# Turning sums and later batches' x on VectorE in 32x32 blocks, in an attention and feed-forward kernel written by a planner

## The chip, the cores and the metric

The kernel runs on one core of one Trainium2 chip. The metric is the device time in microseconds (us). A core has TensorE (PE; matmuls, its weight loads are shown as PEld), VectorE (DVE), ScalarE (ACT), GpSimd (POOL) and a queue SP that here only issues DMAs. Matmul results land in PSUM, in banks of 512 fp32 columns; everything else lives in SBUF, which has 128 partitions.

## The reference

The input x has 4 batches of 12480 tokens with 128 channels; there are 32 inducing points. The second part is a feed-forward block with 2048 hidden units over all 49920 tokens.

```python
def mab(q, kv):
    s = scale * (q @ kv.transpose(0, 2, 1))
    s = s - s.max(-1, keepdims=True)
    a = np.exp(s)
    a /= a.sum(-1, keepdims=True) + 1e-09
    return a @ kv
h = mab(I, x)          # 32 inducing points attend to all tokens of a batch
y = mab(x, h)          # every token attends to those 32 results
...
h = np.maximum(y @ w_in, 0.0)
out = (h * h @ w_out)
```

## The kernel before

**Tiling.** A unit is 960 tokens (UNIT), 13 units to a batch, 52 in all; a block is half a unit, 480 tokens (BLK). A unit of x is loaded with tokens on 120 partitions, 8 rows of 128 channels on each (tile xn).

**The first attention** (class First). TensorE turns x into channels by tokens, four transposes of 120 tokens for each block (tile xtp in PSUM, L463), and ScalarE or VectorE copies the result to SBUF (tile xt). Then come the first scores (L478), maximum, exponential, a turn of the weights (ep, L512), and the mix with xn (nb, L536), which is added up over the batch with a running maximum. The units of batch 0 are handled before the main part ("early"). The 39 units of batches 1 to 3 are handled inside the main part, each of them 13 units before it is needed.

**The second attention** (class Second) gives each token its weights over the 32 points: scores from xt (na, L674), a copy to SBUF (ss), a turn (s2t, L693), maximum, exponential, sum, division, a turn back (ap, L752). The high part (sw, rounded to fp32r) and the rest are copied out of PSUM, and 16 small DMAs spread them over 128 partitions as the stack st, tokens of a block lying every second 120 of it.

**The feed-forward** (ffn_block). The product of h with w_in is made once per batch (hw), so the hidden units come straight from st: 16 matmuls of 128 x 480 per block (tile h, L896). ScalarE makes relu (L908) and square (L924) into g. VectorE splits g into a rounded part hi (L929) and a rest lo (L934). TensorE then adds hi times wo_hi, hi times wo_lo and lo times wo_hi into one PSUM bank op (L973), 48 matmuls per block. The sum op holds channels by tokens. It is copied to SBUF (ot, by either engine), turned on TensorE in four transposes (otp, L993), copied by VectorE into osb, and a whole unit is stored by one DMA with 4 KB runs. The last block of all is handled in two halves.

**What sets the order.** Nothing is issued as it is written. `add` puts each step into a Plan with an engine (or a choice, "ACT|DVE"), a cost in ns, a due time, what it needs, and the buffers it takes. `Plan.run` goes through the steps as a list scheduler and issues the instructions in that order, so each engine's order is fixed. SP's waits are in its own order too. PERIOD is the planned time of a unit; it spaces the due times.

**PSUM.** Four banks hold h, two hold op (tag o), and two (tag m) are shared by all small products: xtp, na, nb, ep, s2t, ap and otp.

Of the kernel before, what the change touches and what calls it, by code (L numbers as in the profile page):

```python
# [11 lines left out]
F32 = mybir.dt.float32  # L12
# [10 lines left out]
NT = 8  # L23
UNIT = TS * NT
BLK = UNIT // 2


class Task:
# [135 lines left out]
def induced_attention_then_squared_relu_ffn(  # L164
# [16 lines left out]
    scale = 1.0 / math.sqrt(C)  # L181
    NQ = NF // 4
    GB, HB, LB = 3, 2, 2
    PERIOD, START, T_MAIN, NARROW, STEP = 32000.0, 2600.0, 44000.0, -9000.0, 3000.0
    W_DUE = [14e3, 20e3, 28e3, 34e3, 50e3, 52e3, 56e3, 60e3]

    XT, OT, ST = ("ACT|DVE", "ACT|DVE"), ("ACT|DVE", "ACT|DVE"), "ACT|DVE"
# [2 lines left out]
    ORDER = "x0 x1 x2 i0 x3 x4 x5 i1 x6 x7 x8 i2 x9 x10 i3 x11 x12 o0 o1 o2 o3".split()  # L190
    SPARE = (6, 7, 8)
    FIRST_PAIRS, LAST_PAIRS = 2, 1
    OB, SS, SS_NS = "DVE", "DVE", 317

    FUSED = set()
    POOL_HI = set()
# [4 lines left out]
    HALVES = True  # L201
    PATIENCE = (0.0, 0.0, 40.0)

    PAIR, PAIR_DUE, XTP_PAIR = False, 3000.0, False
    MB = 2
    G1_DUE, SQ_DUE, HI_DUE, LO_DUE, OP_DUE = -2000.0, 6000.0, 5000.0, 6000.0, 10500.0
    WIDE_LATER, NEXT_FIRST, STEP_0 = 7000.0, 2000.0, 600.0
# [4 lines left out]

    const = ctx.enter_context(tc.tile_pool(name="const", bufs=1))
    xn_pool = ctx.enter_context(tc.tile_pool(name="xn", bufs=3))
    xt_pool = ctx.enter_context(tc.tile_pool(name="xt", bufs=NU + 1))
    hw_pool = ctx.enter_context(tc.tile_pool(name="hw", bufs=2))
    att = ctx.enter_context(tc.tile_pool(name="att", bufs=2))
# [1 line left out]
    ps_h = ctx.enter_context(tc.tile_pool(name="ps_h", bufs=2, space=PSUM))  # L219
    ps_o = ctx.enter_context(tc.tile_pool(name="ps_o", bufs=4 - MB, space=PSUM))  # L220
    ps_m = ctx.enter_context(tc.tile_pool(name="ps_m", bufs=MB, space=PSUM))
    plan = Plan(dict(xn=3, early=6, xt=NU + 1, m=MB, h=2, o=4 - MB, g=GB, hi=HB, lo=LB, st=2, sw=2), T_MAIN, STICK, PATIENCE)

    def bank(name):
        return ps_m.tile([P, 512], F32, tag="m", name=name)


    x_v = x.rearrange("b (p j) c -> b p j c", p=TS)
    out_v = out.rearrange("(b p j) c -> b p j c", b=B, p=TS)

    def load_x(b, u, pool):
        xn = pool.tile([TS, NT, C], F32, tag="xn", name=f"xn_{b}_{u}")
        nc.sync.dma_start(xn, x_v[b, :, u * NT:(u + 1) * NT, :])
        return xn

    ind_sb = const.tile([M, C], F32, name="ind_sb")
# [32 lines left out]
    def copy(task, dst, src):  # L269
        ENG[task.by](dst, src)  # L270
# [137 lines left out]
    class First:  # L408
        def __init__(self, b, u, due, early=False, begun=None):

            self.b, self.u, self.early, self.n, self.begun = b, u, early, f"{b}_{u}", begun
            self.s = s = state.setdefault(b, {"xt": {}, "chain": None, "bxt": {}})
            self.home = "early" if early and u not in SPARE else "xn"
            self.bx = Buffer(self.home)
            self.bt = s["bxt"][u] = Buffer("xt")
            lead = 2500 if early else 8000

            def load():
                self.xn = (pools["early"] if self.home == "early" else xn_pool).tile(
                    [TS, NT, C], F32, tag="xn", name=f"xn_{self.n}"  # L420
                )
                nc.sync.dma_start(self.xn, x_v[b, :, u * NT:(u + 1) * NT, :])

            loaded = add("SP", 2050, load, ORDER.index(f"x{u}") * 10.0 - 1000.0 if b == 0 else due - lead - 20000, takes=[self.bx], late=0)
            self.turned = []
            if XTP_PAIR and not early:
                self.turn_both(due - lead, loaded)
                return
            for k in range(2):
                self.turned.append(self.turn(k, due - lead + k * lead * 0.4, loaded))  # L430

        def turn_both(self, due, loaded):
            banks = [Buffer("m"), Buffer("m")]
            tp = {}

            def turn():
                self.xt = self.s["xt"][self.u] = xt_pool.tile([C, UNIT], F32, tag="xt", name=f"xt_{self.n}")
                for k in range(2):
                    tp[k] = bank(f"xtp_{self.n}_{k}")
                    for t in range(4):  # L440
                        nc.tensor.transpose(tp[k][:, t * TS:(t + 1) * TS], self.xn[:, 4 * k + t, :], ident[:TS, :TS])

            t = state["turn"] = add("PE", 750, turn, due, [loaded, state.get("turn"), self.begun], mode="t",
                                    takes=banks + [self.bt], reads=[self.bx])
            for k in range(2):
                def turned(k=k):
                    copy(self.turned[k], self.xt[:, k * BLK:(k + 1) * BLK], tp[k][:, :BLK])

                self.turned.append(add(XT[k], (440, 567), turned, due + XT_DUE, [t], reads=[banks[k], self.bt]))

        def turn(self, k, due, loaded):
            bank_ = Buffer("o" if self.early else "m")
# [212 lines left out]
    class Second:  # L665
# [13 lines left out]
        def weigh(self, scored, where, bank_, due, step, pair=None):  # L679
# [119 lines left out]
            if first:  # L799
# [5 lines left out]
                for k in range(2):  # L805
# [2 lines left out]
                    last = add(ST, (455, 565), lambda k=k: stacked1(k), d + (5 + k) * step, [t, last],  # L808
                               takes=[] if k else [self.bst], reads=[ba] + ([self.bst] if k else []))
                    t1.append(last)  # L810
                self.ready = t1
                return
            t = add("PE", 219, back, d + 4 * step, [tp], takes=[ba], mode="t")
            th = add(ST, (255, 317), high, d + 5 * step, [t], takes=[bw], reads=[ba])
# [60 lines left out]
    def ffn_block(b, u, k, second, t0, g_open, by_pairs, fused, bulk):  # L875
# [7 lines left out]
        def quad(j, last):  # L883
# [4 lines left out]
            for i in range(2):  # L888
# [3 lines left out]
                def wide(l, i=i, c=c):  # L892
                    if l == 0:
                        c["hp"] = ps_h.tile([P, 2, 512], F32, tag="h", name=f"h_{n}_{2 * j + i}")
                    f = 4 * j + 2 * i + l
                    nc.tensor.matmul(  # L896
                        c["hp"][:, l, :BLK].rearrange("p (q t) -> p q t", q=Q), s["hw"][:, f * P:(f + 1) * P], s["st", u][:, :, k, :],
                        start=True, stop=True,
                    )

# [82 lines left out]
        for j in range(NQ):  # L983
            last = quad(j, last)

        def done():
            w["ot"] = att.tile([P, BLK], F32, tag="ot", name=f"ot_{n}")
            copy(td, w["ot"], w["op"][:, :BLK])

        def turn():  # L990
            w["tp"] = tp = bank(f"otp_{n}")
            for q in range(Q):
                nc.tensor.transpose(  # L993
                    tp[:TS, q * P:(q + 1) * P], w["ot"][:, q * TS:(q + 1) * TS], ident
                )

        def turned():
            if k == 0:
                s["osb", u] = att.tile([TS, NT, C], F32, tag="osb", name=f"osb_{b}_{u}")

            copy(
                tt, s["osb", u].rearrange("t (q k) c -> t k q c", k=2)[:, k],
                w["tp"][:TS, :].rearrange("t (q c) -> t q c", q=Q),
            )

        def store():
            nc.sync.dma_start(out_v[b, :, u * NT:(u + 1) * NT, :], s["osb", u])

        def store_block():
            pair = out_v[b, :, u * NT:(u + 1) * NT, :].rearrange("t (q k) c -> t k q c", k=2)  # L1010
            nc.sync.dma_start(pair[:, k], s["osb", u].rearrange("t (q k) c -> t k q c", k=2)[:, k])

        end = t0 + PERIOD / 2 + 8000
        if HALVES and (b, u) == units[-1] and k == 1:

            for h in range(2):
                def done_h(h=h):
                    if h == 0:
                        w["ot"] = att.tile([P, BLK], F32, tag="ot", name=f"ot_{n}")
                    c = slice(h * 2 * TS, (h + 1) * 2 * TS)  # L1020
                    ENG["ACT" if h else "DVE"](w["ot"][:, c], w["op"][:, c])

                def turn_h(h=h):
                    w["tp", h] = tp = bank(f"otp_{n}_{h}")
                    for q in range(2):
                        nc.tensor.transpose(
                            tp[:TS, q * P:(q + 1) * P], w["ot"][:, (2 * h + q) * TS:(2 * h + q + 1) * TS], ident
                        )

                def rows(x, h=h):  # L1030
                    return x.rearrange("t (q k) c -> t k q c", k=2)[:, k, 2 * h:2 * h + 2]

                def turned_h(h=h, rows=rows):
                    ENG["ACT" if h else "DVE"](
                        rows(s["osb", u]), w["tp", h][:TS, :2 * P].rearrange("t (q c) -> t q c", q=2)
                    )

                def store_h(rows=rows):
                    nc.sync.dma_start(rows(out_v[b, :, u * NT:(u + 1) * NT, :]), rows(s["osb", u]))

                bt = Buffer("m")
                e = "ACT" if h else "DVE"
                t = add(e, 300, done_h, end + h, [last], reads=[bo], late=0)
                t = add("PE", 219, turn_h, end + 600, [t], takes=[bt], mode="t")
                t = add(e, 330, turned_h, end + 1500, [t], reads=[bt], late=0)
                add("SP", 1500, store_h, end + 6000, [t])
            return w["begun"]
        bt = Buffer("m")
        td = add(OT[k], (455, 570), done, end + OT_DUE, [last], reads=[bo], late=LATE_OT)
        t = add("PE", 437, turn, end + OTP_DUE, [td], takes=[bt], mode="t")  # L1050
        t = tt = s["out", u, k] = add(OB, (480, 600), turned, end + OSB_DUE, [t], reads=[bt])
        if (b, u) == units[-1]:
            add("SP", 1500, store_block, end + 6000, [t])
        elif k == 1:
            add("SP", 2000, store, end + 6000, [t, s["out", u, 0]])
        return w["begun"]


# [73 lines left out]
```

## Time and profile before

| what | value |
|---|---|
| time, median of three runs | 1729.77 us (1728.26 to 1730.32) |
| profiled execution, its span | 1730.0 us |
| TensorE busy | 1706.0 us, 99% |
| VectorE busy | 1651.4 us, 95% |
| ScalarE busy | 1605.6 us, 93% |
| GpSimd busy | 58.3 us, 3% |
| DMA | 82.06 MB in 56935 packets; 18.1% of 16 engines |

The span is the time of the one execution that the profiler recorded. Busy is the time in which an engine had an instruction running; overlapping records count once. Idle time is put down to whatever ended it, the releaser. In a group, "out<-in" are the program's tile names, x is a count, then come busy microseconds and the mean duration in nanoseconds of one instruction. Copies by the helper all have line L270, so they are told apart by tile.

### The profile page before, as it was taken

The numbers are of one execution on the slowest core, as the hardware profiler recorded it, in microseconds if no ns is written. First come the engines' busy times: TensorE is split into PE (matmuls) and PEld (weight loads), VectorE is DVE, ScalarE is ACT, GpSimd is POOL, SyncE is SP. The second block draws the span as 40 slices with busy tenths as digits, with TensorE's granted clock in tenths as the row PEclk, the third lists the DMA queues.
The fourth block names the chain that finished last, engine by engine and source line by source line (L and its number), as shares of the span: only waits on it lengthen the run. The fifth ranks groups of instructions, "written<-read, shape, count | busy, mean of one in ns | idle before, by whom it ended". The sixth has DMA issues, their size and how long they took to land.

```text
span 1730.0 us, 25326 instructions
## 1 busy us (share of the span) xinstructions
PE 1706.0 (99%) x9527; PEld 1416.2 (82%) x9527; DVE 1651.4 (95%) x1734; ACT 1605.6 (93%) x1686; POOL 58.3 (3%) x57
## 2 busy tenths in 40 slices
PE   7899999999999999999999999999999999999998
PEld 5588888888788888888878888888887888888887
DVE  5999999999999999999999999999999999999998
ACT  6699999999989999999988999999998999999997
POOL 0000000000000000000000000000000000000000
PEclk9899999999999999999999999999999999999999
DMA  9121111111121111111212111111110111111010
GB/s 234 51 55 47 51 43 44 52 45 43 36 57 47 50 43 46 52 45 43 53 29 58 49 43 47 51 44 44 42 28 24 35 35 40 30 37 33 24 46 23
DMA packets 56935, 82.06 MB, mean 47 GB/s; under 512 B 14790, under 2 KB 43942, under 8 KB 56814
## 3 DMA queue, kind: packets, MB, share of 16 engines
q1 hardware_dynamic: 56814, 80.46, 18.1%
q8 instruction: 75, 1.23, 0.3%
q14 instruction: 46, 0.38, 0.1%
HBM read 29.77 MB, written 25.56 MB: 32 GB/s over the span
## 4 chain that ended last, share of the span: by engine, by line
PE 94%; DVE 2%; ACT 1%; DMA 1%; SPq 1%; issue 0%; ACTq 0%; DVEq 0%
PE op L973 61%; PE h L896 21%; PE otp L993 3%; PE xtp L463 2%; PE na L674 2%; PE nb L536 1%; PE na L478 1%; PE ep L512 1%; PE s2t L693 1%; PE ap L752 1%; PE wp L632 1%; DVE lo L934 0%; SPq L768 0%; DVE hi L929 0%; PE sp L478 0%
## 5 line engine op out<-in xcount | busy, mean ns | idle before, releaser
L934 DVE TENSOR_TENSOR lo<-g,hi 128x1920 fp32r<-128x1920 f32 (+1 forms) x419 | 895.2, 2137 | 16.8 <-DVE hi L929 0.5
L908 ACT ACTIVATE g<-h 128x960 f32<-128x960 f32 x832 | 794.7, 983 | 62.5 <-PE h L896 60.8
L924 ACT ACTIVATE g<-g 128x1920 f32<-128x1920 f32 (+1 forms) x419 | 758.8, 1811 | 4.0
L896 PE MATMUL h<-st,hw 128*128 128x480 f32 x1664 | 523.5, 392 | 2.4 <-DMA st<-sw 1.2
L929 DVE CAST hi<-g 128x1920 fp32r<-128x1920 f32 (+1 forms) x419 | 480.0, 1146 | 20.0 <-PE op L973 9.6
L973 PE MATMUL op<-hi,wo_lo 128*128 128x480 f32 x1664 | 495.7, 383 | 0.0
L973 PE MATMUL op<-hi,wo_hi 128*128 128x480 f32 x1664 | 458.8, 386 | 0.0
L973 PE MATMUL op<-lo,wo_hi 128*128 128x480 f32 x1664 | 436.6, 382 | 0.0
L973 PEld LDWEIGHTS op<-lo,wo_hi 128*128 128x128 f32 x1664 | 311.4, 188 | 52.6 <-issue 1.0
L973 PEld LDWEIGHTS op<-hi,wo_lo 128*128 128x128 f32 x1664 | 308.9, 188 | 53.0 <-issue 4.6
L896 PEld LDWEIGHTS h<-st,hw 128*128 128x128 f32 x1664 | 303.0, 189 | 57.1 <-issue 11.7
L973 PEld LDWEIGHTS op<-hi,wo_hi 128*128 128x128 f32 x1664 | 304.1, 188 | 45.9 <-issue 0.9
L715 POOL TENSOR_SCALAR z<-z 120x8 f32<-120x8 f32 x51 | 57.6, 1130 | 1606.6 <-DVE z L711 1606.6
L270 DVE COPY osb<-otp 120x512 f32<-120x512 f32 x103 | 70.2, 682 | 0.1
L463 PE MATMUL xtp<-ident,xn 120*128 120x120 f32 x416 | 61.9, 276 | 4.3 <-DMA xn<-in_x_dram 3.6
L463 PEld LDWEIGHTS xtp<-ident,xn 120*128 120x128 f32 x416 | 51.2, 146 | 17.5 <-issue 3.7
L993 PE MATMUL otp<-ident,ot 128*120 128x128 f32 x412 | 61.8, 272 | 0.5 <-DVE ot L270 0.5
L993 PEld LDWEIGHTS otp<-ident,ot 128*120 128x120 f32 x412 | 50.4, 137 | 12.8 <-DVE ot L270 1.5
L270 ACT COPY xt<-xtp 128x480 f32<-128x480 f32 x71 | 40.3, 572 | 13.4 <-PE xtp L463 13.4
L270 ACT COPY ot<-op 128x480 f32<-128x480 f32 x65 | 37.1, 570 | 0.8 <-PE op L973 0.8
L536 PE MATMUL nb<-xn,et 120*32 120x128 f32 x752 | 34.1, 280 | 0.0
L674 PE MATMUL na<-xt,hT 128*32 128x240 f32 x416 | 32.7, 387 | 0.4 <-DVE hT L270 0.4
(117 smaller groups left out, 650.6 us busy)
## 6 DMA issues: line engine op xcount, KB each, us to landing
xn<-in_x_dram SPq DMA_DIRECT2D x52, 480.0 KB, 4.3
st<-sw SPq DMA_DIRECT2D x816, 30.0 KB, 1.9
out_dram<-osb SPq DMA_DIRECT2D x51, 480.0 KB, 3.4
hi_i<-in_moe_w_in_dram SPq DMA_DIRECT2D x2, 512.0 KB, 13.5
lo_i<-in_moe_w_in_dram SPq DMA_DIRECT2D x2, 512.0 KB, 15.6
hi_o<-in_moe_w_out_dram SPq DMA_DIRECT2D x2, 512.0 KB, 11.9
lo_o<-in_moe_w_out_dram SPq DMA_DIRECT2D x2, 512.0 KB, 9.8
out_dram<-osb SPq DMA_DIRECT2D x1, 240.0 KB, 2.6
```

Source lines behind the costliest of these rows:

```text
L270: ENG[task.by](dst, src)
L463: nc.tensor.transpose(v["tp"][:, t * TS:(t + 1) * TS], self.xn[:, 4 * k + t, :], ident[:TS, :TS])
L536: nc.tensor.matmul(where[q * M:(q + 1) * M, :], self.et[:, k, q * M:(q + 1) * M], self.xn[:, 2 * q + k, :], start=(k == 0), stop=(k == 1),)
L674: nc.tensor.matmul(where[q * M:(q + 1) * M, :], self.s["hT"][:, :M], self.s["xt"][self.u][:, q * 2 * TS:(q + 1) * 2 * TS], start=True, sto ...
L715: E.tensor_scalar(v["z"], v["z"], 1e-9, 0.0, ALU.add, ALU.add)
L896: nc.tensor.matmul(c["hp"][:, l, :BLK].rearrange("p (q t) -> p q t", q=Q), s["hw"][:, f * P:(f + 1) * P], s["st", u][:, :, k, :], start=Tr ...
L908: nc.scalar.activation(g, h, AF.Relu)
L924: nc.scalar.activation(v["g"][:, h], v["g"][:, h], AF.Square)
L929: ENG[by](v["hi"][:, h], v["g"][:, h])
L934: engine.tensor_sub(v["lo"][:, h], v["g"][:, h], v["hi"][:, h])
L973: nc.tensor.matmul(w["op"][:, :BLK], wo[:, 4 * j + l, :], v[name][:, l, :], start=(j == x == 0 and l == 0), stop=(j == NQ - 1 and x == 5 a ...
L993: nc.tensor.transpose(tp[:TS, q * P:(q + 1) * P], w["ot"][:, q * TS:(q + 1) * TS], ident)
```

## The change

1. VectorE turns op straight out of PSUM, in 32x32 blocks, into a tile ob (one instruction of 480 columns per block). The copies ot and osb, the transposes otp and their bank go. In ob, partition 32g + t, row r, holds 32 channels of group g of token 32r + t, so four DMAs, one for each group, store a block in runs of 32 channels (128 bytes).
2. For units of batches 1 to 3, x is loaded a second time, by four DMAs in runs of 128 bytes, into a tile xb (one buffer) with that same arrangement, and one VectorE instruction of 960 columns turns it into xt. The transposes xtp and their copies stay for batch 0 alone. The mix still reads xn.
3. Blocks of 32 tokens must be consecutive, so the order of tokens in a unit changes: xn is loaded with token j x 120 + p of the unit on partition p (runs of 512 bytes where they were 4 KB), and a block's tokens stand side by side in st, so a hidden product reads one run of 480 columns. The first unit's two blocks now both wait for both halves of its stack.
4. The copy ss of the second scores may go to ScalarE or VectorE.
5. PERIOD goes from 32000 to 30500 ns.

The last block's two halves are now two VectorE turns, of 256 and 224 columns, with four DMAs each. An unused variant (turn_both) goes.

```diff
+S = 32
+NR = BLK // S
...
-    PERIOD, START, T_MAIN, NARROW, STEP = 32000.0, 2600.0, 44000.0, -9000.0, 3000.0
+    PERIOD, START, T_MAIN, NARROW, STEP = 30500.0, 2600.0, 44000.0, -9000.0, 3000.0
...
-    OB, SS, SS_NS = "DVE", "DVE", 317
+    OB, SS, SS_NS = "DVE", "ACT|DVE", (255, 317)
...
+    xb_pool = ctx.enter_context(tc.tile_pool(name="xb", bufs=1))
...
-    x_v = x.rearrange("b (p j) c -> b p j c", p=TS)
-    out_v = out.rearrange("(b p j) c -> b p j c", b=B, p=TS)
+    xb_v = x.rearrange("b (u r t) (g c) -> b u g t r c", r=UNIT // S, t=S, c=S)
+    x_v = x.rearrange("b (u j p) c -> b u p j c", j=NT, p=TS)
+    out_v = out.rearrange("(b u k r t) (g c) -> b u k g t r c", b=B, k=2, t=S, r=NR, g=P // S)
...
-            if XTP_PAIR and not early:
-                self.turn_both(due - lead, loaded)
+            if not early:
+                self.turned.append(self.turn_blocks(due - lead))
                 return
...
+        def turn_blocks(self, due):
+            b, u = self.b, self.u
+            bb = Buffer("xb")
+            v = {}
+
+            def load():
+                v["xb"] = xb_pool.tile([P, UNIT // S, S], F32, tag="xb", name=f"xb_{self.n}")
+                for g in range(P // S):
+                    nc.sync.dma_start(v["xb"][g * S:(g + 1) * S], xb_v[b, u, g])
 
             def turn():
...
+                self.xt = self.s["xt"][u] = xt_pool.tile([C, UNIT], F32, tag="xt", name=f"xt_{self.n}")
+                nc.vector.transpose(self.xt, v["xb"].rearrange("p r c -> p (r c)"))
+
+            t = state["blocks"] = add("SP", 2050, load, due - 20000, [state.get("blocks")], takes=[bb], late=0)
+            t = state["turn"] = add("DVE", 1070, turn, due + XT_DUE, [t, state.get("turn"), self.begun], takes=[self.bt], reads=[bb])
+            return t
...
-                self.ready = t1
+                self.ready = [last] * 2
...
-                        c["hp"][:, l, :BLK].rearrange("p (q t) -> p q t", q=Q), s["hw"][:, f * P:(f + 1) * P], s["st", u][:, :, k, :],
+                        c["hp"][:, l, :BLK], s["hw"][:, f * P:(f + 1) * P],
+                        s["st", u][:, 2 * k:2 * k + 2].rearrange("p q k t -> p (q k t)"),
...
-        td = add(OT[k], (455, 570), done, end + OT_DUE, [last], reads=[bo], late=LATE_OT)
-        t = add("PE", 437, turn, end + OTP_DUE, [td], takes=[bt], mode="t")
-        t = tt = s["out", u, k] = add(OB, (480, 600), turned, end + OSB_DUE, [t], reads=[bt])
...
+        def turn(rows):
+            if "ob" not in w:
+                w["ob"] = att.tile([P, NR, S], F32, tag="ob", name=f"ob_{n}")
+            nc.vector.transpose(
+                w["ob"][:, rows].rearrange("p r c -> p (r c)"), w["op"][:, rows.start * S:rows.stop * S]
             )
...
+        def store(rows):
+            for g in range(P // S):
+                nc.sync.dma_start(out_v[b, u, k, g, :, rows], w["ob"][g * S:(g + 1) * S, rows])
...
+        parts = [slice(0, 8), slice(8, NR)] if (b, u) == units[-1] and k == 1 else [slice(0, NR)]
+        t = None
+        for rows in parts:
+            t = add("DVE", 70 + 500 * (rows.stop - rows.start) / NR, lambda rows=rows: turn(rows), end + OT_DUE, [last, t],
+                    reads=[bo], late=LATE_OT if len(parts) == 1 else 0)
+            add("SP", 2000, lambda rows=rows: store(rows), end + 6000, [t])
```

More of the change, by code (lines that the diff above doesn't have):

```diff
@@ L202, in induced_attention_then_squared_relu_ffn @@
     PATIENCE = (0.0, 0.0, 40.0)
-    PAIR, PAIR_DUE, XTP_PAIR = False, 3000.0, False
+    PAIR, PAIR_DUE = False, 3000.0
     MB = 2
@@ L221, in induced_attention_then_squared_relu_ffn @@
     ps_m = ctx.enter_context(tc.tile_pool(name="ps_m", bufs=MB, space=PSUM))
-    plan = Plan(dict(xn=3, early=6, xt=NU + 1, m=MB, h=2, o=4 - MB, g=GB, hi=HB, lo=LB, st=2, sw=2), T_MAIN, STICK, PATIENCE)
+    plan = Plan(dict(xn=3, xb=1, early=6, xt=NU + 1, m=MB, h=2, o=4 - MB, g=GB, hi=HB, lo=LB, st=2, sw=2), T_MAIN, STICK, PATIENCE)
     def bank(name):
         return ps_m.tile([P, 512], F32, tag="m", name=name)
-    x_v = x.rearrange("b (p j) c -> b p j c", p=TS)
-    out_v = out.rearrange("(b p j) c -> b p j c", b=B, p=TS)
+    xb_v = x.rearrange("b (u r t) (g c) -> b u g t r c", r=UNIT // S, t=S, c=S)
+    x_v = x.rearrange("b (u j p) c -> b u p j c", j=NT, p=TS)
+    out_v = out.rearrange("(b u k r t) (g c) -> b u k g t r c", b=B, k=2, t=S, r=NR, g=P // S)
     def load_x(b, u, pool):
         xn = pool.tile([TS, NT, C], F32, tag="xn", name=f"xn_{b}_{u}")
-        nc.sync.dma_start(xn, x_v[b, :, u * NT:(u + 1) * NT, :])
+        nc.sync.dma_start(xn, x_v[b, u])
         return xn
@@ L421, in load @@
                 )
-                nc.sync.dma_start(self.xn, x_v[b, :, u * NT:(u + 1) * NT, :])
+                nc.sync.dma_start(self.xn, x_v[b, u])
             loaded = add("SP", 2050, load, ORDER.index(f"x{u}") * 10.0 - 1000.0 if b == 0 else due - lead - 20000, takes=[self.bx], late=0)
             self.turned = []
-            if XTP_PAIR and not early:
-                self.turn_both(due - lead, loaded)
+            if not early:
+                self.turned.append(self.turn_blocks(due - lead))
                 return
@@ L430, in __init__ @@
                 self.turned.append(self.turn(k, due - lead + k * lead * 0.4, loaded))
-        def turn_both(self, due, loaded):
-            banks = [Buffer("m"), Buffer("m")]
-            tp = {}
-            def turn():
[L437 to L449, printed above, removed]
+        def turn_blocks(self, due):
[6 more added lines that the diff above has]
+                    nc.sync.dma_start(v["xb"][g * S:(g + 1) * S], xb_v[b, u, g])
+            def turn():
+                self.xt = self.s["xt"][u] = xt_pool.tile([C, UNIT], F32, tag="xt", name=f"xt_{self.n}")
[3 more added lines that the diff above has]
+            return t
         def turn(self, k, due, loaded):
@@ L984, in ffn_block @@
             last = quad(j, last)
[L986 to L1003, printed above, removed]
-            )
@@ L1006, in store @@
[L1006 to L1011, printed above, removed]
-        end = t0 + PERIOD / 2 + 8000
[L1014 to L1047, printed above, removed]
@@ L1048, in ffn_block @@
-        bt = Buffer("m")
-        td = add(OT[k], (455, 570), done, end + OT_DUE, [last], reads=[bo], late=LATE_OT)
-        t = add("PE", 437, turn, end + OTP_DUE, [td], takes=[bt], mode="t")
-        t = tt = s["out", u, k] = add(OB, (480, 600), turned, end + OSB_DUE, [t], reads=[bt])
[L1052 to L1055, printed above, removed]
+        def turn(rows):
[3 more added lines that the diff above has]
+                w["ob"][:, rows].rearrange("p r c -> p (r c)"), w["op"][:, rows.start * S:rows.stop * S]
+            )
```

## The prediction

> **What bounds the kernel now.** First the page: the busy shares and the chain that ended last.
>
> ```profile
> span 1730.0 us, 25326 instructions
> PE 1706.0 (99%) x9527; PEld 1416.2 (82%) x9527; DVE 1651.4 (95%) x1734; ACT 1605.6 (93%) x1686; POOL 58.3 (3%) x57
> PE 94%; DVE 2%; ACT 1%; DMA 1%; SPq 1%; issue 0%; ACTq 0%; DVEq 0%
> ```
>
> TensorE is the bound, but VectorE and ScalarE stand close behind. Averages hide how close, so I cut windows: six ordinary units while later batches' x are still turned, six of the last batch, and the stretch of the first loads.
>
> ```profile
> core 0: us, PE busy (x) PEld busy (x) DVE busy (x) ACT busy (x) POOL busy (x), PEclk, DMA share, GB/s
> 646.00:838.00 192.00, 191.99 (x1091) 161.47 (x1092) 187.22 (x192) 182.31 (x186) 7.07 (x6) 1.00 0.18 47
> 1477.00:1657.00 180.00, 180.00 (x888) 151.26 (x887) 175.40 (x157) 174.21 (x163) 2.41 (x6) 1.00 0.13 34
> 20.00:40.00 20.00, 18.18 (x236) 13.13 (x235) 13.75 (x43) 14.65 (x44) 0.00 (x0) 1.00 1.00 242
> ```
>
> TensorE never pauses in the main part, at full granted clock. A middle unit takes 192/6 = 32.0 us, of which VectorE is busy 187.22/6 = 31.2 and ScalarE 30.4; a unit of the last batch 30.0, VectorE 29.2, ScalarE 29.0. So work taken from TensorE pays one for one only for the first microsecond; after that VectorE decides.
>
> Next, the timeline of TensorE shows what a turn costs it (start, duration, instruction).
>
> ```profile
> 803.40 0.60 PE L993 MATMUL otp<-ident,ot 128*120 128x128 f32 x4
> 803.76 0.68 PE L896 MATMUL h<-st,hw 128*128 128x480 f32 x2
> 804.28 0.60 PE L973 MATMUL op<-hi,wo_lo 128*128 128x480 f32 x2
> ...
> 806.19 0.68 PE L896 MATMUL h<-st,hw 128*128 128x480 f32 x2
> ...
> 826.87 0.57 PE L463 MATMUL xtp<-ident,xn 120*128 120x120 f32 x4
> 827.20 1.12 PE L973 MATMUL op<-hi,wo_hi 128*128 128x480 f32 x4
> 828.16 0.59 PE L973 MATMUL op<-hi,wo_lo 128*128 128x480 f32 x2
> 828.60 0.60 PE L896 MATMUL h<-st,hw 128*128 128x480 f32 x2
> ...
> 838.26 0.61 PE L896 MATMUL h<-st,hw 128*128 128x480 f32 x2
> ```
>
> Read starts, not durations, since matmuls overlap. Two wide products go by in 0.44 us (828.16 to 828.60). The output turn takes 0.36 us to the next start, and the pair behind it 0.52 instead of 0.44: 0.44 in all. The x turn takes 0.33, and the four products behind it 0.96 instead of 0.88: 0.41. The rows at 806.19 and 838.26 are first products of two units, 32.07 apart.
>
> **The change part by part.**
>
> *TensorE.* Each unit loses two output turns, 2 x 0.44 = 0.88 us, in all 52 units. The 39 units that bring in x of batches 1 to 3 also lose two x turns, 2 x 0.41 = 0.82; batch 0 keeps its own. A middle unit then needs 32.0 - 1.70 = 30.3 us of TensorE, a last one 30.0 - 0.88 = 29.1. In sum 52 x 0.88 + 39 x 0.82 = 78 us: were nothing else in the way, 1730 - 78 = 1652. The hidden products' right side becomes one run of 480 instead of four of 120. I cost that at nothing: two h products (828.60 row's kind) go at the pace of two op products that already read such a run.
>
> *VectorE.* Its timeline, and its groups in the same six units:
>
> ```profile
> 802.30 0.65 DVE L270 COPY ot<-op 128x480 f32<-128x480 f32 x1
> 802.87 2.15 DVE L934 TENSOR_TENSOR lo<-g,hi 128x1920 fp32r<-128x1920 f32 x1
> ...
> 809.05 0.40 DVE L270 COPY ss<-na 128x240 f32<-128x240 f32 x1
> 809.36 0.15 DVE L497 SCALAR_TENSOR_TENSOR neg<-mx,neg 128x1 f32<-128x1 f32 x1
> ...
> 827.48 0.66 DVE L270 COPY xt<-xtp 128x480 f32<-128x480 f32 x1
> 828.05 2.15 DVE L934 TENSOR_TENSOR lo<-g,hi 128x1920 fp32r<-128x1920 f32 x1
> ```
> ```profile
> L934 DVE TENSOR_TENSOR lo<-g,hi 128x1920 fp32r<-128x1920 f32 x48 | 103.1, 2149 | 1.2
> L929 DVE CAST hi<-g 128x1920 fp32r<-128x1920 f32 x48 | 55.4, 1155 | 2.5 <-PE op L973 1.3 <-ACT fade L507 1.2
> L270 DVE COPY osb<-otp 120x512 f32<-120x512 f32 x12 | 8.2, 683 | 0.0
> L270 DVE COPY xt<-xtp 128x480 f32<-128x480 f32 x6 | 3.9, 657 | 0.0
> L270 DVE COPY ot<-op 128x480 f32<-128x480 f32 x6 | 3.9, 650 | 0.0
> ```
>
> Start to start, ot and xt take 0.57 each (0.08 less than recorded), ss 0.31; osb, recorded at 0.683, then takes 0.60. A middle unit loses two osb, one ot and one xt: 2.34 us (the other ot and xt are ScalarE's). It gains two turns of 480 columns and one of 960. No row shows a VectorE turn. Bounds: one element per cycle like the 480-column copy, 0.57, and for 960 its double less what is fixed, 0.57 + 0.50 = 1.07; or the pace halved, 1.07 and 2.07. I take the lower end, since the nearest row is the PSUM copy of the very same tile: 2 x 0.57 + 1.07 = 2.21. Even the cheapest end leaves VectorE's load where it was: 31.2 - 2.34 + 2.21 = 31.07. The Trainium skill, "VectorE: DVE Perf Modes", section "The three transpose paths", gives 311 ns for 128 columns; stretched at its 0.96 GHz that is an estimate of 0.68 and 1.18 us recorded, about 0.60 and 1.10 start to start, and by it the total would be some 4 us above mine. That figure is for a 2-byte type; no run here shows a 4-byte one.
>
> The ss copy may go to ScalarE: 31.07 - 0.31 = 30.76 busy. What of the idle time is VectorE's own? It idles (192 - 187.22)/6 = 0.80 us a unit, of it 2.5/6 = 0.42 waiting for others by the rows above, so 0.38 is its own, between dependent instructions. Upper end of a full VectorE: 30.76 + 0.38 = 31.1. Lower end: TensorE's 30.3, since recorded time overlaps by 0.08 (ot: 0.65 against 0.57) only where instructions run back to back, and closing gaps wins that back. I take the middle, 30.7 a middle unit.
>
> *ScalarE* loses one ot and one xt and may get ss: it falls below 30.4 a unit, so it is not the bound.
>
> *Last batch.* VectorE there loses two osb (1.20; ot was ScalarE's) and gains 1.14: still about 29.2, or 28.9 without ss, against 29.1 on TensorE. I take 29.2, which is 0.8 less than now.
>
> *DMAs and the SP queue.*
>
> ```profile
> 824.08 11.76 SPq L768 DMA_DIRECT2D st<-sw  x16
> ```
> ```profile
> st<-sw SPq DMA_DIRECT2D x816, 30.0 KB, 1.9
> ...
> out_dram<-osb SPq DMA_DIRECT2D x1, 240.0 KB, 2.6
> out_dram<-osb SPq DMA_DIRECT2D x2, 120.0 KB, 2.0
> ```
>
> A unit issues 16 spreads, one x load and one store now; then 16, one x load, four block loads and eight stores: 29 instead of 18. At the spreads' 11.76/16 = 0.74 each, the eleven more cost at most 8.1 us of a queue that is engaged about 13 of 32: hidden. Both new kinds move 128-byte runs: 960 x 4 loaded and as many stored, 7680 packets a unit over 16 engines. Price of one: rows of 512 bytes appear in the last block's stores, where 240 rows more (480 against 240) land 0.6 us later, 15 an engine, so at most 40 ns; by bytes alone a quarter, 10. I take 20: 480 x 20 = 9.6 us of engine time a unit, added to 0.18 x 32 = 5.8: about half the unit, hidden. The block load is due 20 us ahead and its one buffer is free once the last turn is done. Each store waits on SP for its VectorE turn; behind it stand the next loads, all early, and the spreads, which come due before it.
>
> *Start and end.* The first x loads turn from 120 runs of 4 KB into 960 of 512 bytes, while the DMA engines are full (share 1.00). Thirteen loads of 0.48 MB at 242 GB/s are 26 us; the price is between nothing and 64 packets x 40 ns = 2.6 us for each instead of 2.0, so up to 8.
>
> ```profile
> L463 PE MATMUL xtp<-ident,xn 120*128 120x120 f32 x416 | 61.9, 276 | 4.3 <-DMA xn<-in_x_dram 3.6
> ```
>
> TensorE waits 3.6 us in all for x there, so I take 1. The first unit waiting for both halves of its stack costs under 1 (taken as nothing, other setup work lies beside it). At the end two turns and eight issues stand for copies, turns and two issues: taken as even, a microsecond or two either way inside the range.
>
> *Sum*: 1730 - 39 x 1.3 - 13 x 0.8 + 1 = 1730 - 50.7 - 10.4 + 1 = 1670. The profiled span of 1730.0 equals the median of the runs, 1729.77, so nothing is added.
>
> **The rivals.**
>
> 1. *TensorE stays the bound* (the gaps of VectorE close, both ss and the high part of sw go to ScalarE): 1652 to 1656. For it: ScalarE has 1.6 us a unit free, and the banks of the small products lose four of nine users. Against it: VectorE would have to run without its 0.38 us.
> 2. *The turn runs at half pace.* Adds 2 x 0.5 + 1.0 = 2.0 to a middle unit (32.7) and 1.0 to a last (30.2): 1730 + 39 x 0.7 + 13 x 0.2 + 1 = 1761, slower. It decides from about 1.65 cycles an element, where a middle unit is back at 32.0. Against it: every one-input VectorE row from PSUM goes one a cycle.
> 3. *Short packets fill the DMA engines.* 480 x p + about 5 us a unit passes 32 us at p = 56 ns. At 62 (what 960-byte rows cost: a last unit has 0.13 x 30 us x 16 engines for 512 of them and 120 rows of 4 KB, and a middle unit with 0.18 x 32 x 16 for 120 more of 4 KB prices those at 250) a middle unit takes 35: 1730 + 39 x 3 - 10 = 1837, slower. The Trainium skill, "DMA: Bandwidth & Descriptors", section "Specifications", puts line rate at 512 bytes and up, with a read-modify-write below; no run here shows a shorter data row.
> 4. *The stack comes late.* From a unit's first product (806.19) to the last spread landed, 824.08 + 11.76 + about 1.3 (1.9 after its issue begins), are 31.0 us, with 1 us to spare before 838.26. Its steps are paced by due times that mostly stay. If they keep their hours, a unit can't be under 31.0, and one more microsecond behind store packets makes 31.6: 1730 - 39 x 0.4 - 10 = 1704. Against it: fewer users of the banks, and ss on whichever engine is free.
>
> **How the numbers follow.** Forecast with VectorE as the bound: 0.52, its own range 1658 to 1688. Rival 1: 0.27. Rival 4: 0.09. Rival 2: 0.07. Rival 3: 0.05. The range 1650 to 1702 takes in the forecast and rival 1 and most of what lies between forecast and rival 4, and leaves out under 2 in 10. Faster by over 0.2% (3.5 us, about what a measurement of this kernel can tell from no change): forecast and rivals 1 and 4 less a little, 0.86; within 0.2%: 0.03; slower: rivals 2 and 3, 0.11.
>
> **What would show it.** TensorE without xtp after the start and without otp; VectorE turns of about 0.65 (480) and 1.15 (960) recorded; middle units 30.7 apart, last ones 29.2; TensorE no longer unbroken (about 0.4 idle a middle unit, ended by VectorE's hi or lo or by ScalarE's g), VectorE over 98% busy; DMA share near 0.5. Wrong if a turn records over 1 us, if the share passes 0.9, or if h waits for st.

## The result, and the profile after

The changed kernel takes 1678.5 us (median of 4 runs, 1676.8 to 1681.9) against 1730.05: a ratio of 0.9704, 95% interval 0.9693 to 0.9716. The forecast was 1670, range 1650 to 1702. The page of the changed kernel, then its windows over six middle units, six of the last batch and the first loads:

```profile
span 1677.3 us, 24531 instructions
PE 1631.7 (97%) x8799; PEld 1340.5 (80%) x8799; DVE 1608.4 (96%) x1619; ACT 1564.8 (93%) x1657; POOL 77.6 (5%) x57
q1 hardware_dynamic: 451260, 99.66, 33.2%
PE 76%; DVE 12%; issue 5%; ACT 3%; DMA 2%; SPq 2%; DVEq 0%; ACTq 0%
```
```profile
662.00:845.00 183.00, 183.00 (x1015) 152.93 (x1015) 181.71 (x177) 177.47 (x187) 10.52 (x6) 1.00 0.39 68
1428.00:1604.00 176.00, 175.85 (x844) 146.81 (x843) 171.32 (x147) 171.72 (x162) 9.52 (x6) 1.00 0.18 35
20.00:40.00 20.00, 14.89 (x205) 10.62 (x200) 11.94 (x37) 12.79 (x38) 0.00 (x0) 1.00 1.11 220
```

Over these six middle units one takes 183/6 = 30.5 us, a last one about 29.3, and VectorE is busy 99% of the middle stretch. TensorE's share of the chain falls from 94% to 76%; VectorE's rises from 2% to 12%.

The six units end with the last but one of batch 1, which takes 31.4 us and carries steps that come once a batch, so 30.5 is a little too long for an ordinary unit. The second to the eleventh unit of a batch are free of that. The next fence has these ten for batches 0, 1 and 2:

```profile
103.82:411.17 307.35, 306.10 (x1667) 253.32 (x1667) 304.64 (x300) 295.39 (x303) 15.87 (x10) 1.00 0.37 67
510.90:813.59 302.69, 302.69 (x1662) 253.78 (x1660) 300.09 (x291) 294.89 (x311) 16.87 (x10) 1.00 0.38 66
913.11:1216.13 303.02, 303.02 (x1662) 253.27 (x1660) 300.72 (x291) 295.51 (x311) 16.87 (x10) 1.00 0.36 62
```

An ordinary unit takes 30.74 us in batch 0, but 30.27 and 30.30 in batches 1 and 2. First hidden products mark the units (start, duration); first of before, then of after, the start of the main part and of the last batch:

```profile
67.00 1.55 PE L896 MATMUL h<-st,hw 128*128 128x480 f32 x3
...
1329.60 0.38 PE L896 MATMUL h<-st,hw 128*128 128x480 f32 x1
```
```profile
74.67 0.77 PE L899 MATMUL h<-st,hw 128*128 128x480 f32 x1 [0.65 <-ACT st L274]
...
1286.47 0.37 PE L899 MATMUL h<-st,hw 128*128 128x480 f32 x1
```

| stretch | before, us | after, us | moved | forecast |
|---|---|---|---|---|
| start, to the first hidden product | 67.0 | 74.7 | +7.7 | +1 |
| units of the first 3 batches | 1262.6 | 1211.8 | -50.8 | -50.7 |
| last batch and end | 400.4 | 390.9 | -9.5 | -10.4 |

The groups that are new or moved, over the whole run:

```profile
L993 DVE STREAM_TRANSPOSE ob<-op 128x480 f32<-128x480 f32 (+1 forms) x105 | 70.2, 669 | 3.8 <-PE op L977 3.7
L448 DVE STREAM_TRANSPOSE xt<-xb 128x960 f32<-128x960 f32 x39 | 45.6, 1170 | 1.5 <-DMA xb<-in_x_dram 1.5
L274 ACT COPY ss<-na 128x240 f32<-128x240 f32 x52 | 19.4, 374 | 25.0 <-PE na L481 13.9 <-PE na L677 7.9 <-DVE mx L494 3.0
L274 ACT CAST sw<-ap 128x240 fp32r<-128x240 f32 x37 | 14.0, 377 | 2.3 <-PE ap L755 2.2
```

VectorE turns at the pace of a copy: 0.67 us recorded for 480 columns, where the copy ot of the same tile took 0.65, and 1.17 for 960. The planner gave every ss, and 37 instead of 6 high parts of sw, to ScalarE. Of the 14 high parts left on VectorE, nine fall into the ten ordinary units of batch 0 and none into those of batches 1 and 2.

### The profile page after: what moved, and what is told of

Its sections match the earlier page's. It is cut to its first block, busy times and chain, and to the rows that moved or that the text cites. A ratio compares the mean times of both kernels' runs of the same rounds, so it can differ in the third digit from the quotient of the medians.

```text
span 1677.3 us, 24531 instructions
## 1 busy us (share of the span) xinstructions
PE 1631.7 (97%) x8799; PEld 1340.5 (80%) x8799; DVE 1608.4 (96%) x1619; ACT 1564.8 (93%) x1657; POOL 77.6 (5%) x57
## 4 chain that ended last, share of the span: by engine, by line
PE 76%; DVE 12%; issue 5%; ACT 3%; DMA 2%; SPq 2%; DVEq 0%; ACTq 0%
PE op L977 52%; PE h L899 18%; DVE lo L938 5%; DVE hi L933 4%; PE na L677 1%; ACT g L912 1%; SPq L426 1%; PE nb L539 1%; ACT g L928 1%; PE na L481 1%; DMA hi_i<-in_moe_w_in_dram 1%; DMA xn<-in_x_dram 1%; SPq L771 1%; DMA xb<-in_x_dram 1%; PE s2t L696 1%
## 5 line engine op out<-in xcount | busy, mean ns | idle before, releaser
L912 ACT ACTIVATE g<-h 128x960 f32<-128x960 f32 x832 | 786.2, 992 | 30.3 <-PE h L899 18.6
L977 PE MATMUL op<-lo,wo_hi 128*128 128x480 f32 x1664 | 476.4, 383 | 2.8 <-DVE lo L938 2.8
L977 PE MATMUL op<-hi,wo_lo 128*128 128x480 f32 x1664 | 454.1, 382 | 0.0
L718 POOL TENSOR_SCALAR z<-z 120x8 f32<-120x8 f32 x51 | 76.9, 1508 | 1536.5 <-DVE z L714 1536.5
L993 DVE STREAM_TRANSPOSE ob<-op 128x480 f32<-128x480 f32 (+1 forms) x105 | 70.2, 669 | 3.8 <-PE op L977 3.7
L448 DVE STREAM_TRANSPOSE xt<-xb 128x960 f32<-128x960 f32 x39 | 45.6, 1170 | 1.5 <-DMA xb<-in_x_dram 1.5
L274 ACT COPY ss<-na 128x240 f32<-128x240 f32 x52 | 19.4, 374 | 25.0 <-PE na L481 13.9
L539 PEld LDWEIGHTS nb<-xn,et 120*32 120x32 f32 x752 | 25.0, 110 | 7.2 <-issue 0.2
L274 ACT COPY xt<-xtp 128x480 f32<-128x480 f32 x26 | 14.5, 557 | 14.9 <-PE xtp L466 14.9
L515 PE MATMUL ep<-ident,e 128*120 128x128 f32 x104 | 20.7, 281 | 6.3 <-ACT e L507 6.3
L274 ACT COPY et<-ep 120x256 f32<-120x256 f32 x52 | 19.6, 378 | 6.8 <-PE ep L515 6.6
```

The lines of the kernel that those rows point to most:

```text
L448: nc.vector.transpose(self.xt, v["xb"].rearrange("p r c -> p (r c)"))
L539: nc.tensor.matmul(where[q * M:(q + 1) * M, :], self.et[:, k, q * M:(q + 1) * M], self.xn[:, 2 * q + k, :], start=(k == 0), stop=(k == 1),)
L718: E.tensor_scalar(v["z"], v["z"], 1e-9, 0.0, ALU.add, ALU.add)
L912: nc.scalar.activation(g, h, AF.Relu)
L977: nc.tensor.matmul(w["op"][:, :BLK], wo[:, 4 * j + l, :], v[name][:, l, :], start=(j == x == 0 and l == 0), stop=(j == NQ - 1 and x == 5 a ...
L993: nc.vector.transpose(w["ob"][:, rows].rearrange("p r c -> p (r c)"), w["op"][:, rows.start * S:rows.stop * S])
```

## The experiments

All ratios are to the kernel before on the same chip; the changed kernel's is 0.9704. Runs with the same edit in two plans stand together.

**Long x rows at the start.**

```diff
-    x_v = x.rearrange("b (u j p) c -> b u p j c", j=NT, p=TS)
+    x_v = x.rearrange("b (u p j) c -> b u p j c", j=NT, p=TS)
```

> The changed kernel with xn loaded in runs of 4 KB again (8 rows of 128 channels per partition); nothing else differs, so the tokens that xn and the blocks call by the same number are not the same ones: read for time alone. Theory A, the short x rows hold up the full DMA engines at the start: the x loads of batch 0 end near 41 us instead of 46, the first hidden product moves from 74.7 us to 69 to 70, and the time falls by 5 us to about 1673 (ratio to before 0.967). Rival, the start is late for other reasons (the wait for both halves of the first stack, VectorE's order): the first hidden product stays after 73 us, the time within 1.5 us of 1678.5.

Measured 1673.4, ratio 0.9676 (0.9663 to 0.9689). The first product comes at 70.3, and the order of everything is unchanged:

```profile
70.28 0.77 PE L899 MATMUL h<-st,hw 128*128 128x480 f32 x1 [0.65 <-ACT st L274]
...
1280.52 0.37 PE L899 MATMUL h<-st,hw 128*128 128x480 f32 x1
```

Its units of the first three batches take 1280.5 - 70.3 = 1210.2, against 1211.8 in the changed kernel; the 1.6 lie in the first unit of batch 1 (see the clock, last section). So 4.4 of the 7.7 us lost at the start are the 512-byte rows. The changed kernel's own VectorE timeline shows where more of it lies:

```profile
69.34 0.69 DVE L644 TENSOR_TENSOR hw<-wp,hw 64x512 fp32r<-64x512 f32 x1
70.46 1.18 DVE L448 STREAM_TRANSPOSE xt<-xb 128x960 f32<-128x960 f32 x1 [0.42 <-DMA xb<-in_x_dram]
71.56 0.72 DVE L736 TENSOR_TENSOR sk<-d,sk 120x256 fp32r<-120x256 f32 x2
```

The first block turn, for batch 1, stands in front of the last steps (sk) of the first unit's stack and waits for its load: 0.42 + 1.10. Two runs below, each in a plan of its own, bear on that part. The kernel without the second load has its first product at 71.7, 3.0 earlier. The last run, in another order, keeps the second load and has it at 71.7 too; there VectorE does sk before the turn:

```profile
69.42 0.75 DVE L736 TENSOR_TENSOR sk<-d,sk 120x256 fp32r<-120x256 f32 x2
...
71.61 1.18 DVE L448 STREAM_TRANSPOSE xt<-xb 128x960 f32<-128x960 f32 x1
```

So of the 7.7 us, 4.4 are the rows, and about 3.0 come and go with where that turn stands in VectorE's order, not with the load as such. The wait for both halves was not tried by itself; 0.3 are left for it.

**The same with every token in its place.** The copies of batch 0's xt write every eighth column, the first scores read every eighth.

```diff
-                copy(e, self.xt[:, k * BLK:(k + 1) * BLK], v["tp"][:, :BLK])
+                copy(e, self.xt.rearrange("c (p j) -> c j p", j=NT)[:, 4 * k:4 * k + 4, :],
+                     v["tp"][:, :BLK].rearrange("c (j p) -> c j p", j=4))
...
-                    self.xt[:, q * 2 * TS:(q + 1) * 2 * TS], start=True, stop=True,
+                    self.xt.rearrange("c (p j) -> c j p", j=NT)[:, 2 * q:2 * q + 2, :], start=True, stop=True,
```

> As the run before, but with partition p of xn holding tokens 8p to 8p+7 and with what goes with it: the start's copies of xt write every eighth column, and the first scores read every eighth column. Theory A: the start gains the same 5 us, time 1673. The price is in the strided reads and writes: 416 score products at 0.37 us recorded; if a stride of eight columns cost TensorE nothing, 1673; if it doubled them, some 4 x 0.1 us more in each of 52 units, that is 1693.

Measured 1696.4, ratio 0.9808 (0.9795 to 0.9822): near the price named for a doubled score, but put together otherwise: against the run with long rows alone, each of 39 units takes 0.34 us more, and the start is 9.8 us later (first product at 80.1). The groups of the start with the rows contiguous, then strided:

```profile
L274 ACT COPY xt<-xtp 128x480 f32<-128x480 f32 x26 | 14.3, 558 | 11.9 <-PE xtp L466 11.8
...
L481 PE MATMUL sp<-xt,indT 128*32 128x240 f32 x104 | 11.8, 413 | 0.3
```
```profile
L274 ACT COPY xt<-xtp 128x480 f32<-128x480 f32 x26 | 26.1, 1037 | 11.7 <-PE xtp L466 11.7
L482 PE MATMUL sp<-xt,indT 128*32 128x240 f32 x104 | 22.4, 606 | 0.3 <-ACT xt L274 0.3
```

The stride costs more than the long rows give.

**VectorE relieved.** The turn of the sums does 32 of 480 columns: first with a plan that knows it, then in the order of the changed kernel.

```diff
-                w["ob"][:, rows].rearrange("p r c -> p (r c)"), w["op"][:, rows.start * S:rows.stop * S]
+                w["ob"][:, rows.start], w["op"][:, rows.start * S:(rows.start + 1) * S]
...
-                nc.sync.dma_start(out_v[b, u, k, g, :, rows], w["ob"][g * S:(g + 1) * S, rows])
+                nc.sync.dma_start(out_v[b, u, k, g, :, rows], w["ob"][g * S:(g + 1) * S, rows.start:rows.start + 1].broadcast_to([S, rows.stop - rows.start, S]))
...
-            t = add("DVE", 70 + 500 * (rows.stop - rows.start) / NR, lambda rows=rows: turn(rows), end + OT_DUE, [last, t],
+            t = add("DVE", 103, lambda rows=rows: turn(rows), end + OT_DUE, [last, t],
```

> The turn of the sums does 32 of its 480 columns and the stores send those 32 for all (output wrong but for them); the planner is told 103 ns. VectorE is relieved of 2 x 0.47 = 0.93 us a unit, TensorE of nothing. Theory A, VectorE sets the middle unit (30.5 us, busy 99.3%) and TensorE's own 30.3 stands just below: middle unit 30.3, last ones 29.1 instead of 29.4, time 1678.5 - 39 x 0.2 - 13 x 0.3 = 1667. Rival B, TensorE sets it already: no more than 2 us, 1677. Rival C, VectorE's load and not TensorE's is what costs, all through: 1678.5 - 52 x 0.9 = 1632.

Measured 1700.1, ratio 0.9829 (0.9815 to 0.9842): 22 us slower than the changed kernel with 48 us less for VectorE to do. None of the three theories had that. In units of batch 1, VectorE is idle 6% of the time, and so is ScalarE:

```profile
500.00:800.00 300.00, 294.85 (x1569) 238.70 (x1567) 281.80 (x273) 280.47 (x293) 10.91 (x9) 1.00 0.34 61
```

No engine is full there, which leaves the order as what holds up the unit (31.7 us in that batch). Hence the same edit without the last pair of lines, in one order:

> The turn of the sums does 32 of its 480 columns again (the stores send those for all), but the planner is told the old 570 ns, so every engine keeps the order of the changed kernel. VectorE alone is relieved, by 0.93 us a unit. The run with a new plan was slower, 1700, which load can't explain. Theory D, the order was at fault there, and in one order VectorE's load costs: middle units 30.3, TensorE's own need, time about 1667 (at most 1672). Rival B, TensorE sets the time already: within 2 us of 1678.5. Rival E, the turn's shortness itself does harm: near 1700 again.

Measured 1671.7, ratio 0.9663 (0.9650 to 0.9676): 7 us faster, at the weak end of theory D. The same ten units of batches 0, 1 and 2 as in the changed kernel's fence above:

```profile
103.88:407.49 303.61, 303.61 (x1668) 254.68 (x1667) 297.92 (x301) 295.01 (x303) 15.87 (x10) 1.00 0.37 68
504.77:807.18 302.41, 302.41 (x1661) 254.06 (x1660) 294.80 (x291) 295.92 (x311) 16.87 (x10) 1.00 0.39 66
907.30:1209.72 302.42, 302.42 (x1661) 254.05 (x1660) 294.36 (x291) 295.34 (x311) 16.88 (x10) 1.00 0.36 62
```

In batch 0 a unit falls from 30.74 to 30.36 us, about TensorE's own need, as theories A and D have it. In batches 1 and 2 it stood there already, and VectorE's new time to spare (294.80 busy of 302.41) buys nothing.

**TensorE relieved**, in both ways: a pair of products left out of the plan, and the same pair left out with the plan unchanged (shown).

```diff
                         w["op"] = ps_o.tile([P, 512], F32, tag="o", name=f"op_{n}")
+                    if j == 1 and m == 1 and i == 0:
+                        return
```

> One pair of products (hi times wo_lo, second quad) is left out of each block, so TensorE is relieved of 2 x 0.44 = 0.88 us a unit and no other engine of anything; the output lacks that small term. Theory A, VectorE is as full as TensorE: its own lower end is near 30.2, so 1678.5 - 39 x 0.3 - 13 x 0.3 = about 1663. Rival B, TensorE alone sets the time: 1678.5 - 52 x 0.88 = 1633.

Measured 1677.1, ratio 0.9695 (0.9681 to 0.9708): nothing gained.

> The pair of products is left out as before (0.88 us a unit less for TensorE), but the plan still counts it, so every engine keeps the order of the changed kernel. Theory A, VectorE is as full as TensorE: 1678.5 - 52 x 0.2 = 1668, TensorE waiting for lo and hi. Rival B, TensorE alone sets the time: 1678.5 - 46 = 1633. If both hold in turns along the kernel, between them, and more than the 10 us that the relief of VectorE gives.

Measured 1675.4, ratio 0.9684 (0.9670 to 0.9697): 3 us of 46. Rival B, TensorE alone, is out by both. Ten ordinary units take 30.70 us each in batch 0 and 30.23 and 30.27 in batches 1 and 2, as in the changed kernel. What TensorE saves it spends waiting; the window of the six middle units, and the waits of its weight loads from 490 to 1250 us, in this run:

```profile
662.00:845.00 183.00, 182.18 (x995) 147.07 (x994) 181.92 (x178) 177.74 (x187) 10.53 (x6) 1.00 0.38 68
```
```profile
PEld h L899 <- ACT g L912: 20.7, 41, 1.9
PEld op L979 <- DVE hi L933: 12.2, 33, 1.0
PEld op L979 <- DVE lo L938: 8.2, 26, 0.7
```

In the changed kernel the same three rows are 6.9, 1.8 and 1.6 us, so TensorE now waits for ScalarE's g and for VectorE's hi and lo, for g the most. The matmul column still says 182.18 of 183 busy although 5.3 us of matmuls are gone; the weight loads, 21 fewer, fell from 152.93 to 147.07. So "183.00 of 183" was no proof of a full TensorE in the changed kernel either. The Trainium skill, "Trainium Kernel Development and Optimization", section "Performance Expectations", says that matmul busy time is a bad metric because matmuls are pipelined, and this pair of rows agrees.

**One part alone.** First the turn of the sums without the second load, then the second load with the old way out (ot, otp, osb).

```diff
-            if not early:
-                self.turned.append(self.turn_blocks(due - lead))
-                return
```

> VectorE turns the sums, but the second load is left out: all 52 units' x is turned on TensorE as before. PERIOD 31300. TensorE has 32.0 - 0.88 = 31.1 us in a middle unit, VectorE about 0.5 less than in the changed kernel (no 960 columns, one xt copy of 0.57). Theory A: TensorE sets the middle at 31.2, the last units at 29.4 as in the changed kernel: 1678.5 + 39 x 0.7 = 1706. Rival, the two parts help by VectorE's choice alone (fewer copies): as fast as the changed kernel, 1680.

Measured 1698.2, ratio 0.9817 (0.9802 to 0.9832). Units of batch 1 go by at 31.0 to 31.1, TensorE's need. The start is 3.0 us shorter, which I had not reckoned with:

```profile
71.66 0.77 PE L896 MATMUL h<-st,hw 128*128 128x480 f32 x1 [0.20 <-ACT st L274]
```

> The second load with VectorE's turn of x alone: the sums go back through ot, TensorE's turn and osb (512-byte runs in the store, by whole units). PERIOD 31300. TensorE has 32.0 - 0.82 = 31.2 in a middle unit; VectorE 31.2 - 0.57 + 1.07 - 0.31 = 31.4 busy. Theory A, VectorE is the limit: middle 31.6, last 30.0 as before, start as late as in the changed kernel: 1730 + 7 - 39 x 0.4 = 1721. Rival, TensorE is the limit: 1730 + 7 - 39 x 0.8 = 1706.

Measured 1724.9, ratio 0.9972 (0.9960 to 0.9983), 4 us above theory A: the start loses 7 us here too (first product at 74.4), and the 39 units win 17. The parts give 32 and 5 us, together 52.

**Short packets.** Each partition's share of a store or block load becomes one run.

```diff
-    xb_v = x.rearrange("b (u r t) (g c) -> b u g t r c", r=UNIT // S, t=S, c=S)
+    xb_v = x.rearrange("b n c -> b (n c)").rearrange("b (u g t r c) -> b u g t r c", g=P // S, t=S, r=UNIT // S, c=S)
...
-    out_v = out.rearrange("(b u k r t) (g c) -> b u k g t r c", b=B, k=2, t=S, r=NR, g=P // S)
+    out_v = out.rearrange("t c -> (t c)").rearrange("(b u k g t r c) -> b u k g t r c", b=B, k=2, g=P // S, t=S, r=NR, c=S)
```

> The stores of ob and the second loads keep their number, place and bytes, but each partition's share is one run in memory (1920 bytes stored, 3840 loaded) instead of runs of 128 bytes; the tokens are mixed up. Packets fall from 7680 to about 1540 a unit. Theory A, the short packets (14 ns each, DMA share 0.39) are hidden: within 2 us of 1678.5. Rival, they crowd the spreads of the stack or the x loads: 5 us or more faster.

Measured 1677.5, ratio 0.9702 (0.9688 to 0.9717): hidden, although the DMA share of the middle stretch falls from 0.39 to 0.28:

```profile
662.00:845.00 183.00, 183.00 (x1012) 153.35 (x1004) 181.45 (x177) 177.59 (x188) 10.52 (x6) 1.00 0.28 68
```

**ss on VectorE alone.**

```diff
-    OB, SS, SS_NS = "DVE", "ACT|DVE", (255, 317)
+    OB, SS, SS_NS = "DVE", "DVE", 317
```

> The copy ss is VectorE's alone again. It puts 0.31 us a unit back on VectorE and takes 0.27 from ScalarE. Theory A, VectorE has no room: 1678.5 + 52 x 0.3 = about 1694 (at least 1688). Rival B, TensorE sets the time: within 2 us.

Measured 1698.2, ratio 0.9823 (0.9806 to 0.9839). Theory A fits the ordinary units of batches 1 and 2: 30.54 and 30.58 us, 0.27 to 0.28 more than with the choice. Those of batch 0 are as long as in the changed kernel (30.70 against 30.74), and 12.9 of the 20 us lie in the first unit and the last two of each batch. Whether load or order makes these longer was not tried in one order.

**The period, and another order of the same work.**

```diff
-    PERIOD, START, T_MAIN, NARROW, STEP = 30500.0, 2600.0, 44000.0, -9000.0, 3000.0
+    PERIOD, START, T_MAIN, NARROW, STEP = 32000.0, 2600.0, 44000.0, -9000.0, 3000.0
```

> PERIOD is 32000 as before; all else as in the changed kernel. The planner's own end of the plan is 1680.6 us instead of 1670.6. Theory D, the order that the due times make sets the time: 10 us more, about 1688. Rival, due times matter little while every engine is full: within 2 us of 1678.5. A second rival, units are held to the planned period: 52 x 1.5 = 78 us more.

Measured 1683.3, ratio 0.9733 (0.9720 to 0.9746): 5 us of the 10 that theory D named, lost in the first unit and the last two of the batches. Units are not held to the period.

> The same instructions as the changed kernel, other due times: PERIOD 31080, NARROW -9150, STEP 3950, SQ_DUE 1240, HI_DUE 5550, LO_DUE 8550, G1_DUE -2030, OT_DUE 4880, XT_DUE 7990, found by trying many on the planner, whose end of the plan falls from 1670.6 to 1653.9. Theory D, the order holds back what the loads would allow: 1678.5 - 16.7 = 1662, middle units near TensorE's 30.3. Rival A, VectorE's work itself is the limit at 30.5: no lower than 1675.

Measured 1662.3, ratio 0.9611 (0.9598 to 0.9624): as theory D had it to the microsecond, and the fastest version here. (The planner's end gave only half of the change in the run before, so that exactness is luck.) Ordinary middle units stand 30.32 apart, and VectorE does five of them with 150.46 us of 151.5:

```profile
649.63 0.38 PE L899 MATMUL h<-st,hw 128*128 128x480 f32 x1
...
679.95 0.38 PE L899 MATMUL h<-st,hw 128*128 128x480 f32 x1
```
```profile
649.60:801.10 151.50, 151.50 (x831) 127.04 (x830) 150.46 (x146) 147.61 (x156) 10.44 (x5) 1.00 0.36 66
```
```profile
PE 91%; ACT 3%; DMA 2%; DVE 1%; SPq 1%; issue 1%; DVEq 0%; ACTq 0%
```

The last fence is its chain: TensorE's again, at its own need of 30.3 a unit. The profiled executions side by side; "ordinary" are the second to the eleventh unit of a batch, "others" the first and the last two of batches 0 to 2 together:

| us | start | ordinary unit, batches 0, 1, 2 | others | last batch and end |
|---|---|---|---|---|
| before | 67.0 | 32.20, 31.82, 31.80 | 304.4 | 400.4 |
| changed | 74.7 | 30.74, 30.27, 30.30 | 298.7 | 390.9 |
| VectorE relieved, same order | 74.7 | 30.36, 30.24, 30.24 | 296.4 | 390.3 |
| TensorE relieved, same order | 76.8 | 30.70, 30.23, 30.27 | 296.1 | 389.2 |
| new order | 71.7 | 30.30, 30.18, 30.19 | 290.0 | 391.9 |

Of the 17.0 us between changed kernel and new order, 3.0 lie in the start, 4.3 in ordinary units of batch 0, 2.0 in those of batches 1 and 2, and 8.7 in the others; the last batch gives 1.0 back. Not all of it is order in the narrow sense. In batch 0 no high part of sw is left on VectorE in these units, and the durations of its instructions add up to 0.27 us a unit less. And the granted clock, 0.50 for 7.6 us between the first product and the last batch of the changed kernel, is 1.00 there in the new order, worth 3.8 us at most (an estimate, half of 7.6). Nine due times were moved at once; which of them count was not tried.

## Why the prediction was right, and where it was not

*TensorE's bill* held for a middle unit, 1.70 us. Two runs show the floors: 31.0 to 31.1 with the output turn alone (32.0 - 0.88), 30.32 in the new order (32.0 - 1.70). For a last unit, 30.0 to 29.3 was seen, not the full 0.88.

*VectorE's bill* held: a turn at the lower bound, 0.67 and 1.17 recorded. The Trainium skill's figure ("VectorE: DVE Perf Modes", "The three transpose paths"), stretched to an estimate of 0.68 and 1.18, agrees, for a 4-byte type too. Rival 2 is out. VectorE's load fell further than I had it, where the high part of sw moved to ScalarE as well as ss: 300.09/10 = 30.0 busy in batch 1 instead of 30.8, but 30.5 in batch 0, where nine of ten high parts stayed.

*The middle unit*: 30.7 was forecast, because VectorE decides. That is what batch 0 shows: 30.74, VectorE busy 304.64 of 307.35 us; relieved, it lets the unit fall to 30.36, while TensorE relieved leaves it at 30.70. (I had taken the middle of two bounds, so the agreement to 0.04 is luck.) Batches 1 and 2 show rival 1, in its own words, with ss and the high part of sw on ScalarE: 30.27 and 30.30, TensorE's floor. There the relief of either engine wins 0.06 at most, since the other, and ScalarE with 97%, is as full. So the step "after that VectorE decides" holds for a third of these units, and which engine decides seems to hang on a choice of the planner that the forecast left open: where the high part of sw goes. That choice was not varied by itself. VectorE's idle time, 0.27 us a unit in batch 0, is below the 0.38 that I had called its own. The sign I named, 0.4 us of idle TensorE a unit, was 0.13 in batch 0 and nothing in batches 1 and 2 by the matmul row.

*The sum over 39 units*, -50.8 against -50.7, is luck. The 30 ordinary ones win 45.1 us, where 30 x 1.3 = 39 were forecast, and the nine others 5.7 instead of 11.7. What the batch changes cost had no term in the forecast; in the new order the nine take 8.7 us less.

*The planned period* got no step of its own in the forecast; it is worth 5 us, by the order it makes.

*DMAs*: hidden, as forecast. Share 0.39 in the middle, where I expected near 0.5: 0.39 x 30.5 x 16 = 190 us a unit, less 32 for the spreads and 38 for x, leaves about 16 ns for a 128-byte packet (an estimate; the trace's own packet records average 14, and I took 20). My sum had kept the 4 KB rows of stores and loads that are no longer there. Rival 3 is out. The Trainium skill ("DMA: Bandwidth & Descriptors", "Specifications") puts a read-modify-write below 512 bytes; stores in long runs show no cost of it in time. Rival 4 is out too: after the first hidden product, which waits 0.6 us for a copy into its own stack, no product waits for st in the changed kernel's list of waits on TensorE, whose longest entries are x at the start (8.9 us), ep (6.3) and g (6.2).

*The start* is the term that was mis-sized: +7.7 for +1, so 6.7 of the 8.5 us between forecast and result. I had bounded the short x rows by 8 and taken 1, because TensorE waits 3.6 us in all for x. That row told how long TensorE waits now, not how much there is to lose: with the DMA engines full, the first loads moved 220 GB/s where they had moved 242. The long rows give back 4.4. About 3.0 more are a turn of x that the forecast counted for every unit alike, and that for batch 1's first unit stood before the first unit's sk.

## What to carry to other kernels

When three engines are each within a few per cent of full and a fixed order is written ahead, a single engine's load no longer gives the time: try another order and another sharing of the work before you shorten an instruction, and try an edit in an unchanged order before you judge it. Cut windows where units begin, and batch by batch: the mean of six units, 30.5, told neither the 30.74 of one batch nor the 30.3 of the other two. Judge a stretch in which the DMA engines are full by what its packets cost, not by how long an engine now waits for them. And check a full matmul row against the waits of the weight loads.

## What the runs showed of the hardware

A 128-byte packet costs a DMA engine about 14 ns by the packet records, 16 by the share of the middle stretch, and 91 x 3840 of them cost nothing measurable where the engines had room, while 512-byte rows in thirteen loads cost 4.4 us where they had none. A column stride of 8 nearly doubles a ScalarE copy's write (558 to 1037 ns) and adds half to a TensorE score's read (413 to 606 ns). GpSimd's 120 x 8 step on z takes 1.51 us on average instead of 1.13 (76.9 us for 51); what slows it was not tried.

TensorE's granted clock is not always full. In the changed kernel it is 0.50, among other stretches at the start, for 6.8 us around the first hidden product, and later for 3.4 us in the first unit of batch 1. The run with long packets has the same order and the full clock in that second stretch; the changed kernel first, then that run:

```profile
491.90:495.30 3.40, 3.40 (x10) 2.85 (x9) 3.40 (x5) 3.40 (x4) 0.00 (x0) 0.50 0.23 35
```
```profile
491.90:495.30 3.40, 3.37 (x15) 2.92 (x16) 3.40 (x5) 3.40 (x4) 0.00 (x0) 1.00 0.15 37
```

Ten matmuls fall into it in place of 15, and the unit takes 29.2 us instead of 27.7. In both runs TensorE was busy for half of the 3.4 us before, 1.71 and 1.73, so what sets the lower clock off is not shown. With ss on VectorE alone it is 0.50 for 14.0 us between the first product and the last batch.
